# Loading half of W2 ahead of batch 1's v, regrouping the plain blocks of the first chunk, and spreading VectorE's sums of W2

## The chip, the cores and the metric

One core of one Trainium2 chip. The metric is the device time of one execution in microseconds (us). The kernel before takes 278.25 us (median of four runs, 277.8 to 278.66).

Engines by their names in the profile: PE is TensorE, DVE VectorE, ACT ScalarE, POOL GpSimd, SP the engine that here only issues DMAs.

## The reference, cut to what matters

```python
q_s = softmax(q over the head dimension);  k_s = softmax(k over the sequence)
kv = einsum('bhsd,bhse->bhde', k_s, v)            # 8 batches, 8 heads, 576 x 64
x  = einsum('bhsd,bhde->bhse', q_s, kv)           # -> 4608 tokens x 512
h  = x @ w_in                                     # 512 -> 2048
out = (h * sigmoid(h)) @ w_out                    # 2048 -> 512
```

## The kernel before

The tokens go through in chunks of 512. "Chunk 0" is the first (576 wide in its first product, so that batch 0 is whole). A chunk has two products: `mm1` with w_in in 16 blocks, each followed by SiLU (tanh on ScalarE, then a product on VectorE), and the product with w_out (W2). Chunk 0 takes the second product plainly, 16 blocks of four matmuls. From chunk 1 on it is done with seven half-size products instead of eight (the Winograd form of Strassen's scheme), which need sums of the activations (S1 to S4, made for each chunk) and sums of W2 (T1 to T4, made once). T3 overwrites a part of W2.

```python
def t_op(i, eng, f0=0, f1=HF):               # a half of one sum of W2: 128 x 1024 fp16
    o, in0, in1 = {1: (T1, B12, B11), 2: (T2, B22, T1), 3: (T3, B22, B12), 4: (T4, B21, T2)}[i]
    f = slice(f0, f1)
    eng.tensor_tensor(out=o[:, f], in0=in0[:, f], in1=in1[:, f], op=ALU.subtract)

def qnorm(b, cc, eng):                       # row scaling of batch b's softmax of q; GpSimd for most
    ...
    eng.tensor_tensor(out=e, in0=e, in1=r[...].to_broadcast(...), op=ALU.mult)

def silu(t, fb, i, o, w):
    ...
    nc.scalar.activation(out=s, in_=i, func=ACT.Tanh, scale=OS)
    nc.vector.scalar_tensor_tensor(out=o, in0=s, scalar=1.0, in1=i, op0=ALU.add, op1=ALU.mult)   # i is in PSUM

# loads issued by GpSimd, cast to the matmul's types on the way
...
load_w2(0, 4)
load(1, "vt", v, 0, nc.gpsimd)
load(1, "vt", v, 1, nc.gpsimd)
load_w2(4, 8)
...
# TensorE's order: "units"; a plan attaches other work ahead of a unit
units += [lambda i=i: mm2_plain(0, i) for i in range(8)]
for i in range(8, NFB):
    units += [a1[i - 8], lambda i=i: mm2_plain(0, i)]
units += a1[NFB - 8:]                        # a1: the 16 mm1 blocks of chunk 1
...
plan(b1 + 13, lambda: t_op(2, nc.vector, 0, 4))      # b1: the first plain block
plan(b1 + 14, lambda: t_op(2, nc.vector, 4, 8))
plan(b1 + 16, lambda: t_op(4, nc.vector, 0, 4))
plan(b1 + 18, lambda: t_op(4, nc.vector, 4, 8))
...
plan(begin[2] + 5, lambda: t_op(3, nc.vector, 0, 4)) # begin[2]: chunk 2's first mm1 block
plan(begin[2] + 8, lambda: t_op(3, nc.vector, 4, 8))
```

The mm1 blocks of chunk 2 go through three PSUM banks in turn: block n cannot start before VectorE has finished the SiLU product of block n-3.

The softmax here doesn't subtract the row's maximum and nothing guards it: scores larger than these inputs give would overflow.

Of the kernel before, what the change touches and what calls it, by code (L numbers as in the profile page):

```python
# [8 lines left out]
FP32 = mybir.dt.float32  # L9
BF16 = mybir.dt.bfloat16  # L10
FP16 = mybir.dt.float16
ACT = mybir.ActivationFunctionType
# [5 lines left out]
def kernel(  # L18
# [9 lines left out]
    nc = tc.nc  # L28
    B, H, S, D = q.shape
    DM, DFF = w_in.shape  # L30
    NT = B * S
    P = 64
    J = S // P
    NG = H // 2
    NC = DM // 128
    NFB = DFF // 128
# [7 lines left out]
    OS = 0.5 / XS  # L44
# [9 lines left out]
    mp = ctx.enter_context(tc.tile_pool(name="mp", bufs=2))  # L54
# [18 lines left out]
    PS = ps.tile([128, 8, 512], FP32, name="PS")  # L73
# [11 lines left out]
    def copy(eng, o, i):  # L85
        if eng is nc.scalar:
            eng.copy(out=o, in_=i)  # L87
        else:
            eng.tensor_copy(o, i)  # L89

    def load(b, name, src, cc, eng):
        t = ld.tile([128, 2, J * D], FP32, name=name)
        st[b][name, cc] = t
        x = src[b].rearrange("(g r) (p j) d -> g (r p) (j d)", r=2, j=J)
        eng.dma_start(out=t, in_=x.rearrange("g x y -> x g y")[:, 2 * cc:2 * cc + 2, :])

    def jgd(b, name, cc):
        return st[b][name, cc].rearrange("p g (j d) -> p j g d", d=D)

    def half(t, cc):  # L100
        return t[:, :, cc * 128:(cc + 1) * 128].rearrange("p j (g d) -> p j g d", d=D)
# [6 lines left out]
    def exp_k(b, cc):  # L108
        nc.scalar.activation(out=half(ek, cc), in_=jgd(b, "kt", cc), func=ACT.Exp)  # L109

    def vcast(b, cc, eng, g0=0, g1=2):
        o = vaug[:, :, 2 * cc + g0:2 * cc + g1, 0:D]
        i = jgd(b, "vt", cc)[:, :, g0:g1, :]
        copy(eng, o, i)
# [13 lines left out]
    def qsum_end(b, cc):  # L128
        new_zq(b)
        nc.vector.reduce_sum(out=st[b]["zq"][:, cc], in_=st[b]["t2", cc], axis=AX.X)  # L130
        nc.vector.reciprocal(out=st[b]["rzq"][:, cc], in_=st[b]["zq"][:, cc])

    def new_zq(b):
        if "zq" not in st[b]:
            st[b]["zq"] = ap.tile([128, 2, J, 2], FP32, name="zq", bufs=2)
            st[b]["rzq"] = ap.tile([128, 2, J, 2], FP32, name="rzq", bufs=2)
# [11 lines left out]
    def qnorm(b, cc, eng):  # L148
        e = half(st[b]["eq"], cc)
        r = st[b]["rzq"][:, cc]  # L150
        eng.tensor_tensor(  # L151
            out=e, in0=e, in1=r[:, :, :, None].to_broadcast([128, J, 2, D]), op=ALU.mult
        )

    def new_qt(b):
        if "qT" not in st[b]:
            st[b]["qT"] = ap.tile([128, J, 2, 128], BF16, name="qT", bufs=2)
        return st[b]["qT"]

    def q_transpose(b):  # L160
        nc.sync.dma_start_transpose(
            out=new_qt(b).rearrange("x j c y -> x (j c) y"),
            in_=st[b]["eq"].rearrange("x j c -> x (j c)"),
        )

    def tr(b, cc, j0, j1, bank):
        t = PS[:, bank, :].bitcast(BF16)
        for j in range(j0, j1):
            nc.tensor.transpose(
                out=t[:, (j - j0) * 128:(j - j0 + 1) * 128],  # L170
                in_=st[b]["eq"][:, j, cc * 128:(cc + 1) * 128],
                identity=ident,
            )
# [5 lines left out]
    def kv(b, cc):  # L179
        for j in range(J):  # L180
            for r in range(2):
                for s in range(2):
                    nc.tensor.matmul(  # L183
                        out=PS[s * 64:(s + 1) * 64, 6 + r, cc * 128:cc * 128 + E1],
                        lhsT=ek[r * 64:(r + 1) * 64, j, (2 * cc + s) * D:(2 * cc + s + 1) * D],
                        rhs=vaug[r * 64:(r + 1) * 64, j, 2 * cc + s, :],
                        start=(j == 0),
                        stop=(j == J - 1),
                    )
# [13 lines left out]
    def kv_both(b):  # L203
        kv(b, 0)
        kv(b, 1)
        kvcopy(b)
# [25 lines left out]
    def xt(t, cc, eng=nc.scalar):  # L232
        got = pieces(t)
        for b, col, n, dst in got:
            xt_mm(b, cc, col, n, 6, dst)
        xt_evac(t, cc, 6, got[0][3], TCH, got[0][3], eng)
# [30 lines left out]
    hb = [0, 2]  # L267
# [27 lines left out]
    def store(t, col, o):  # L295
        for i in range(2):
            nc.sync.dma_start(out=rows(t, col + i * P), in_=o[i * P:(i + 1) * P, :])

    def mm2_plain(t, fc):
        for tb in range(4):  # L300
            nc.tensor.matmul(  # L301
                out=PS[:, 2 + tb, :],
                lhsT=GTS[t % 2][:, fc, tb * 128:(tb + 1) * 128],
                rhs=W2[:, fc, :],
                start=(fc == 0),
                stop=(fc == NFB - 1),
            )

    def mm2_plain_out(t):
        for ms in ((0, 1), (2, 3)):  # L310
            ow = mp.tile([128, 2, DM], FP32, name="ow", bufs=3)
            for i, m in enumerate(ms):
                if i == 0:
                    nc.scalar.activation(out=ow[:, i], in_=PS[:, 2 + m], func=ACT.Copy, scale=OS)
                else:
                    nc.vector.tensor_scalar_mul(out=ow[:, i], in0=PS[:, 2 + m], scalar1=OS)
                store(t, m * 128, ow[:, i])



# [17 lines left out]
    def t_op(i, eng, f0=0, f1=HF):  # L338
        o, in0, in1 = {
            1: (T1, B12, B11),  # L340
            2: (T2, B22, T1),
            3: (T3, B22, B12),
            4: (T4, B21, T2),
        }[i]
        f = slice(f0, f1)
        eng.tensor_tensor(out=o[:, f], in0=in0[:, f], in1=in1[:, f], op=ALU.subtract)  # L346
# [97 lines left out]
    def load_w2(f0, f1):  # L444
        nc.gpsimd.dma_start(
            out=W2[:, f0:f1, :],
            in_=w_out[f0 * 128:f1 * 128, :].rearrange("(fc p) o -> p fc o", p=128),
        )
# [13 lines left out]
    load(1, "kt", k, 0, nc.gpsimd)  # L462
    load(1, "kt", k, 1, nc.gpsimd)
    load_w2(0, 4)
    load(1, "vt", v, 0, nc.gpsimd)
    load(1, "vt", v, 1, nc.gpsimd)
    load_w2(4, 8)

    qnorm(0, 0, nc.vector)
    qsum(0, 1)  # L470
# [33 lines left out]
    units = []  # L504
    at = {}

    def plan(u, f):
        at.setdefault(u, []).append(f)
# [7 lines left out]
    begin = {1: len(units)}  # L516
# [18 lines left out]
    ORDER = (1, 5, 6, 2, 7, 4, 3)  # L535
    a1 = a_units(1)

    units += [lambda i=i: mm2_plain(0, i) for i in range(8)]
    for i in range(8, NFB):
        units += [a1[i - 8], lambda i=i: mm2_plain(0, i)]  # L540
    units += a1[NFB - 8:]
    for t in range(2, NCH):
        begin[t] = len(units)
        bs = b_units(t - 1, ORDER)
# [72 lines left out]
    b1 = begin[1]  # L617
# [10 lines left out]
    plan(15, lambda: exp_k(1, 1))  # L628
    plan(b1, lambda: (tr(1, 0, 0, 5, 6), tr(1, 0, 5, J, 7)))
    plan(b1, lambda: (trcopy(1, 0, 0, 5, 6, nc.scalar), trcopy(1, 0, 5, J, 7)))  # L630
    plan(b1, lambda: (vcast(1, 0, nc.scalar), qsum_end(1, 1), qnorm(1, 1, nc.vector)))
    plan(b1, lambda: load_w2(12, 16))
    plan(b1, lambda: nc.gpsimd.tensor_copy(GTS[1][:, :, 0:64], GTS[0][:, :, TCH:S]))
    plan(b1, lambda: (load(2, "kt", k, 0, nc.gpsimd), load(2, "kt", k, 1, nc.gpsimd)))
    plan(b1 + 2, lambda: (vcast(1, 1, nc.scalar, 0, 1), vcast(1, 1, nc.vector, 1, 2)))
    plan(b1 + 5, lambda: kv_both(1))
    plan(b1 + 5, lambda: (load(2, "vt", v, 0, nc.gpsimd), load(2, "vt", v, 1, nc.gpsimd)))
    plan(b1 + 6, lambda: (xt(1, 0), tr(1, 1, 0, 5, 0), tr(1, 1, 5, J, 1)))
    plan(b1 + 6, lambda: (trcopy(1, 1, 0, 5, 0, nc.scalar), trcopy(1, 1, 5, J, 1)))
    plan(b1 + 7, lambda: xt(1, 1))  # L640

    plan(b1 + 6, lambda: t_op(1, nc.vector, 0, 4))
    plan(b1 + 7, lambda: t_op(1, nc.vector, 4, 8))
    for i, x in enumerate((8, 10)):
        plan(b1 + x, lambda i=i: exp_q(2, i))
        plan(b1 + x + 1, lambda i=i: qsum(2, i, 0))
        plan(b1 + x + 2, lambda i=i: (qsum(2, i, 1), qnorm(2, i, nc.gpsimd)))
        plan(b1 + x + 5, lambda i=i: exp_k(2, i))
    plan(b1 + 12, lambda: q_transpose(2))
    plan(b1 + 13, lambda: t_op(2, nc.vector, 0, 4))  # L650
    plan(b1 + 14, lambda: t_op(2, nc.vector, 4, 8))
    plan(b1 + 16, lambda: t_op(4, nc.vector, 0, 4))
    plan(b1 + 18, lambda: t_op(4, nc.vector, 4, 8))
    for i, x in enumerate((17, 19)):
        plan(b1 + x, lambda i=i: vcast(2, i, nc.scalar))
    plan(b1 + 20, lambda: loads(3, nc.sync))
    plan(b1 + 21, lambda: kv_both(2))
    plan(b1 + 24, lambda: (mm2_plain_out(0), hb.__setitem__(0, 2), hb.__setitem__(1, 3)))
    for i, x in enumerate((24, 26)):
        plan(b1 + x, lambda i=i: xt(2, i))  # L660
    plan(begin[2] + 5, lambda: t_op(3, nc.vector, 0, 4))
    plan(begin[2] + 8, lambda: t_op(3, nc.vector, 4, 8))

    for t in range(2, NCH - 1):
        b = t + 1
# [58 lines left out]
```

## Time and profile before

I use two lengths, read from TensorE's timeline. **Chunk 1** is the time from the first plain block to the first half-size product with W2. **Chunk 2** is the time from there to the same point one chunk later. Later chunks repeat with 27.78 us.

| | kernel before |
|---|---|
| first plain block / first product / next chunk's | 32.97 / 68.47 / 97.42 us |
| chunk 1 | 35.50 us |
| chunk 2 | 28.95 us, 1.17 over 27.78 |
| TensorE busy | 263.3 us, 95% |

The page of the kernel before. "Busy" is followed by its share of the span. Part 4 is the chain of work that ended last:

```profile
span 276.5 us, 5769 instructions
PE 263.3 (95%) x2343; PEld 168.2 (61%) x2372; DVE 200.5 (73%) x291; ACT 160.3 (58%) x239; POOL 67.3 (24%) x60
...
PE 75%; DMA 9%; DVE 8%; issue 4%; POOL 1%; ACT 1%; POOLq 0%
```

TensorE is the bound, so only its waits can be won. TensorE's timeline of the kernel before, at the three points of the table (the lines from 32.97, 68.47 and 97.42) and at its longest waits in the stretch that the change touches (start, length, what, and in brackets the idle time just before and who ended it):

```profile
32.97 3.62 PE L301 MATMUL PS<-W,GT 128*128 128x512 f16 x16
38.12 1.02 PE L301 MATMUL PS<-W,GT 128*128 128x512 f16 x4 [1.53 <-DMA W<-in_moe_w_out_dram]
...
53.95 0.92 PE L272 MATMUL PS<-XT,W 128*128 128x448 bf16 x4 [1.70 <-DVE GT L245]
...
68.47 1.04 PE L362 MATMUL PS<-W,GT 128*128 128x256 f16 x8
...
80.58 1.02 PE L272 MATMUL PS<-XT,W 128*128 128x512 bf16 x4 [0.66 <-DVE GT L245]
...
82.67 0.81 PE L272 MATMUL PS<-XT,W 128*128 128x512 bf16 x3 [0.19 <-DVE GT L245]
...
97.42 1.04 PE L362 MATMUL PS<-W,GT 128*128 128x256 f16 x8
```

The first wait (38.12) is of the fifth plain block: it waits for W2's second quarter, which by the trace's landing records came at 38.08, after the two loads of v (34.24 and 35.70). The others wait for SiLU products (L245) on VectorE. VectorE's timeline at the same places shows why they are late. L346 is a sum of W2; x2 means two halves merged:

```profile
50.33 3.03 DVE L346 TENSOR_TENSOR T<-W,T 128x1024 f16<-128x1024 f16 x2
...
53.82 0.68 DVE L346 TENSOR_TENSOR T<-W,T 128x1024 f16<-128x1024 f16 x1
...
77.58 2.35 DVE L346 TENSOR_TENSOR W<-W 128x1024 f16<-128x1024 f16 x1
```

And GpSimd's timeline there (L151 is the row scaling, L89 the cast of v):

```profile
48.03 4.18 POOL L151 TENSOR_TENSOR eq<-eq,rzq 128x1152 bf16<-128x1152 bf16 x2 [8.69 <-DVE rzq L146]
75.19 4.19 POOL L151 TENSOR_TENSOR eq<-eq,rzq 128x1152 bf16<-128x1152 bf16 x2 [22.98 <-DVE rzq L146]
79.33 3.71 POOL L89 CAST vaug<-vt 128x1152 bf16<-128x1152 f32 x2
```

A half of a sum takes 0.68 us when GpSimd is idle. The first half of T2 (from 50.33) took 2.43 us and ended 0.55 us after GpSimd's scaling (52.22). The second half of T3 (from 77.58) took 2.35 us and ended 0.55 us after it (79.38). So the sum waits for GpSimd's instruction and only then runs. This is what the Trainium skill tells in "SBUF — State Buffer", section "SBUF: two separate sides": VectorE and GpSimd share a pair of SBUF ports, held for a whole instruction by a GpSimd operation or by a VectorE one with two SBUF inputs (the latter against a GpSimd operation that reads SBUF, as the scaling and the cast do). The trace agrees, by the times above.

### The profile page before, as it was taken

The numbers are of one execution on the slowest core, as the hardware profiler recorded it, in microseconds if no ns is written. First come the engines' busy times: TensorE is split into PE (matmuls) and PEld (weight loads), VectorE is DVE, ScalarE is ACT, GpSimd is POOL, SyncE is SP. The second block draws the span as 40 slices with busy tenths as digits, with TensorE's granted clock in tenths as the row PEclk, the third lists the DMA queues.
The fourth block names the chain that finished last, engine by engine and source line by source line (L and its number), as shares of the span: only waits on it lengthen the run. The fifth ranks groups of instructions, "written<-read, shape, count | busy, mean of one in ns | idle before, by whom it ended". The sixth has DMA issues, their size and how long they took to land.

```text
span 276.5 us, 5769 instructions
## 1 busy us (share of the span) xinstructions
PE 263.3 (95%) x2343; PEld 168.2 (61%) x2372; DVE 200.5 (73%) x291; ACT 160.3 (58%) x239; POOL 67.3 (24%) x60
## 2 busy tenths in 40 slices
PE   8899979799989999999999999999999999999993
PEld 3467634345656566656665666566656665666782
DVE  2867766967998489848984898489937674767643
ACT  5767927777844576457645774577464446444410
POOL 1744960500190009000900090009100000000003
PEclk9999999999999999999999999999999999999999
DMA  7999999599758376937792869241225003300444
GB/s 252 312 201 358 307 284 337 155 305 369 206 147 273 79 175 205 295 80 173 203 297 64 195 196 281 73 104 35 53 44 111 2 0 76 78 0 0 95 98 114
DMA packets 35498, 45.85 MB, mean 166 GB/s; under 512 B 16208, under 2 KB 20048, under 8 KB 35472
## 3 DMA queue, kind: packets, MB, share of 16 engines
q1 hardware_dynamic: 29568, 33.69, 44.3%
q0 software_dynamic: 5584, 11.54, 16.0%
q8 instruction: 18, 0.29, 0.4%
q10 hardware_dynamic: 320, 0.26, 0.3%
q14 instruction: 8, 0.07, 0.1%
HBM read 36.70 MB, written 9.44 MB: 167 GB/s over the span
## 4 chain that ended last, share of the span: by engine, by line
PE 75%; DMA 9%; DVE 8%; issue 4%; POOL 1%; ACT 1%; POOLq 0%
PE PS L272 36%; PE PS L362 34%; DMA W<-in_moe_w_out_dram 5%; DMA W<-in_moe_w_in_dram 4%; PE PS L301 2%; PE PS L222 2%; DVE GT L245 2%; PE PS L183 2%; DVE S L336 1%; POOL W L439 1%; DVE T L346 1%; DVE W L346 1%; DVE zq L144 1%; DVE zq L142 1%; DVE rzq L146 0%
## 5 line engine op out<-in xcount | busy, mean ns | idle before, releaser
L245 DVE SCALAR_TENSOR_TENSOR GT<-sg,PS 128x512 f16<-128x512 f32 (+2 forms) x144 | 96.4, 678 | 54.5 <-ACT sg L244 53.9
L244 ACT ACTIVATE sg<-PS 128x512 f32<-128x512 f32 (+2 forms) x144 | 85.8, 598 | 82.6 <-PE PS L272 75.8
L272 PE MATMUL PS<-XT,W 128*128 128x512 bf16 (+1 forms) x484 | 123.6, 375 | 3.9 <-DVE GT L245 2.6
L272 PEld LDWEIGHTS <-W 128*128 128x128 bf16 x512 | 49.9, 98 | 41.7 <-issue 4.0
L362 PEld LDWEIGHTS <-S 128*128 128x128 f16 x512 | 49.2, 98 | 16.6 <-issue 1.2
L151 POOL TENSOR_TENSOR eq<-eq,rzq 128x1152 bf16<-128x1152 bf16 x13 | 27.4, 2118 | 113.3 <-ACT sg L244 81.6
L362 PEld LDWEIGHTS <-GT 128*128 128x128 f16 x384 | 37.1, 98 | 13.1 <-issue 1.2
L362 PE MATMUL PS<-W,S 128*128 128x256 f16 x256 | 33.0, 273 | 0.1
L362 PE MATMUL PS<-W,GT 128*128 128x256 f16 x256 | 32.7, 273 | 0.1
L362 PE MATMUL PS<-T,S 128*128 128x256 f16 x256 | 32.7, 273 | 0.0
L336 DVE TENSOR_TENSOR S<-GT 128x2048 f16<-128x2048 f16 (+1 forms) x17 | 24.3, 1427 | 0.0
L87 ACT CAST XT<-PS 128x1024 bf16<-128x1024 f32 (+2 forms) x18 | 17.3, 962 | 5.7 <-PE PS L222 5.7
L586 POOL DMA_DIRECT2D out_dram<-ow x4 | 2.2, 550 | 75.7 <-DVE ow L571 75.7
L106 ACT ACTIVATE eq<-qt 128x1152 bf16<-128x1152 f32 x16 | 18.6, 1164 | 2.5 <-DMA qt<-in_q_dram 2.5
L109 ACT ACTIVATE ek<-kt 128x1152 bf16<-128x1152 f32 x16 | 18.6, 1165 | 1.4 <-DMA kt<-in_k_dram 1.4
L142 DVE TENSOR_REDUCE zq<-eq 128x18 f32<-128x1152 bf16 x12 | 16.1, 1344 | 3.8 <-ACT eq L106 3.8
L301 PE MATMUL PS<-W,GT 128*128 128x512 f16 x64 | 16.0, 379 | 1.5 <-DMA W<-in_moe_w_out_dram 1.5
L252 PE MATMUL PS<-XT,W 128*128 128x288 bf16 x128 | 16.5, 286 | 0.7 <-DVE GT L245 0.4
L89 POOL CAST vaug<-vt 128x1152 bf16<-128x1152 f32 x10 | 16.7, 1700 | 0.0
L362 PE MATMUL PS<-T,GT 128*128 128x256 f16 x128 | 16.5, 273 | 0.0
L252 PEld LDWEIGHTS <-W 128*128 128x128 bf16 x128 | 12.4, 98 | 4.7 <-issue 1.7
L336 DVE TENSOR_TENSOR S<-GT,S 128x2048 f16<-128x2048 f16 x8 | 13.1, 1641 | 0.0
(58 smaller groups left out, 158.8 us busy)
## 6 DMA issues: line engine op xcount, KB each, us to landing
out_dram<-ow SPq DMA_DIRECT2D x64, 128.0 KB, 2.4
qt<-in_q_dram SPq DMA_DIRECT2D x12, 576.0 KB, 4.8
kt<-in_k_dram SPq DMA_DIRECT2D x12, 576.0 KB, 6.9
vt<-in_v_dram SPq DMA_DIRECT2D x12, 576.0 KB, 7.6
qt<-in_q_dram POOLq DMA_DIRECT2D x4, 576.0 KB, 13.5
kt<-in_k_dram POOLq DMA_DIRECT2D x4, 576.0 KB, 13.2
vt<-in_v_dram POOLq DMA_DIRECT2D x4, 576.0 KB, 13.6
W<-in_moe_w_out_dram POOLq DMA_DIRECT2D x4, 512.0 KB, 14.6
```

The costliest lines, as they stand in the source:

```text
L87: eng.copy(out=o, in_=i)
L106: nc.scalar.activation(out=half(st[b]["eq"], cc), in_=jgd(b, "qt", cc), func=ACT.Exp)
L109: nc.scalar.activation(out=half(ek, cc), in_=jgd(b, "kt", cc), func=ACT.Exp)
L142: nc.vector.reduce_sum(out=z, in_=e, axis=AX.X)
L151: eng.tensor_tensor(out=e, in0=e, in1=r[:, :, :, None].to_broadcast([128, J, 2, D]), op=ALU.mult)
L244: nc.scalar.activation(out=s, in_=i, func=ACT.Tanh, scale=OS)
L245: nc.vector.scalar_tensor_tensor(out=o, in0=s, scalar=1.0, in1=i, op0=ALU.add, op1=ALU.mult)
L252: nc.tensor.matmul(out=PS[:, 2 * (fb % 3) + n, 0:S // 2], lhsT=W1[:, c, fb * 128:(fb + 1) * 128], rhs=XTS[0][:, c, n * (S // 2):(n + 1) * ...
L272: nc.tensor.matmul(out=PS[:, bank, o0:TCH], lhsT=W1[:, c, fb * 128:(fb + 1) * 128], rhs=XTS[t % 2][:, c, o0:TCH], start=(c == 0), stop=(c ...
L301: nc.tensor.matmul(out=PS[:, 2 + tb, :], lhsT=GTS[t % 2][:, fc, tb * 128:(tb + 1) * 128], rhs=W2[:, fc, :], start=(fc == 0), stop=(fc == N ...
L336: nc.vector.tensor_tensor(out=SS[i - 1][:, f], in0=in0[:, f], in1=in1[:, f], op=op)
L362: nc.tensor.matmul(out=PS[:, bank, m * HN:(m + 1) * HN], lhsT=a[:, fc, m * 128:(m + 1) * 128], rhs=bb[:, fc, :], start=(first and fc == 0) ...
```

## The change

The intent: let W2's second quarter land before TensorE asks for it, use the time in which v is then late for two more plain blocks, leave ten mm1 blocks of chunk 1 as a dense closing stretch, take v's cast for batch 2 off ScalarE, and place the sums of W2 where VectorE seems to have room, after the row sums. No arithmetic is added or removed. The diff's core (cut: the plan lines that move with the new order, among them those of batch 1's casts and batch 2's loads, and the split of the plain output into two halves):

```diff
     load_w2(0, 4)
+    load_w2(4, 8)
     load(1, "vt", v, 0, nc.gpsimd)
     load(1, "vt", v, 1, nc.gpsimd)
-    load_w2(4, 8)
 ...
-    units += [lambda i=i: mm2_plain(0, i) for i in range(8)]
-    for i in range(8, NFB):
-        units += [a1[i - 8], lambda i=i: mm2_plain(0, i)]
-    units += a1[NFB - 8:]
+    units += [lambda i=i: mm2_plain(0, i) for i in range(10)]
+    for i in range(10, NFB):
+        units += [a1[i - 10], lambda i=i: mm2_plain(0, i)]
+    units += a1[NFB - 10:]
 ...
-    plan(b1 + 5, lambda: kv_both(1))
+    plan(b1 + 7, lambda: kv_both(1))
 ...
-    plan(b1 + 13, lambda: t_op(2, nc.vector, 0, 4))
-    plan(b1 + 14, lambda: t_op(2, nc.vector, 4, 8))
-    plan(b1 + 16, lambda: t_op(4, nc.vector, 0, 4))
-    plan(b1 + 18, lambda: t_op(4, nc.vector, 4, 8))
-    for i, x in enumerate((17, 19)):
-        plan(b1 + x, lambda i=i: vcast(2, i, nc.scalar))
+    for i, x in enumerate((16, 18)):
+        plan(b1 + x, lambda i=i: (exp_k(2, i), vcast(2, i, nc.gpsimd)))
+    plan(b1 + 18, lambda: t_op(2, nc.vector, 0, 4))
+    plan(b1 + 20, lambda: t_op(2, nc.vector, 4, 8))
 ...
-    plan(begin[2] + 5, lambda: t_op(3, nc.vector, 0, 4))
-    plan(begin[2] + 8, lambda: t_op(3, nc.vector, 4, 8))
+    plan(begin[2] + 7, lambda: t_op(4, nc.vector, 0, 4))
+    plan(begin[2] + 8, lambda: t_op(4, nc.vector, 4, 8))
+    plan(begin[2] + 12, lambda: t_op(3, nc.vector, 0, 4))
+    plan(begin[2] + 13, lambda: t_op(3, nc.vector, 4, 8))
```

More of the change, by code (lines that the diff above doesn't have):

```diff
@@ L307, in mm2_plain, with mm2_plain_out @@
             )
-    def mm2_plain_out(t):
-        for ms in ((0, 1), (2, 3)):
-            ow = mp.tile([128, 2, DM], FP32, name="ow", bufs=3)
-            for i, m in enumerate(ms):
-                if i == 0:
-                    nc.scalar.activation(out=ow[:, i], in_=PS[:, 2 + m], func=ACT.Copy, scale=OS)
-                else:
-                    nc.vector.tensor_scalar_mul(out=ow[:, i], in0=PS[:, 2 + m], scalar1=OS)
-                store(t, m * 128, ow[:, i])
+    def mm2_plain_out(t, ms):
+        ow = mp.tile([128, 2, DM], FP32, name="ow", bufs=3)
+        for i, m in enumerate(ms):
+            if i == 0:
+                nc.scalar.activation(out=ow[:, i], in_=PS[:, 2 + m], func=ACT.Copy, scale=OS)
+            else:
+                nc.vector.tensor_scalar_mul(out=ow[:, i], in0=PS[:, 2 + m], scalar1=OS)
+            store(t, m * 128, ow[:, i])
     WG = [dict() for _ in range(NCH)]
@@ L630 @@
     plan(b1, lambda: (trcopy(1, 0, 0, 5, 6, nc.scalar), trcopy(1, 0, 5, J, 7)))
-    plan(b1, lambda: (vcast(1, 0, nc.scalar), qsum_end(1, 1), qnorm(1, 1, nc.vector)))
+    plan(b1, lambda: (qsum_end(1, 1), qnorm(1, 1, nc.vector)))
     plan(b1, lambda: load_w2(12, 16))
+    plan(b1, lambda: (load(2, "kt", k, 0, nc.gpsimd), load(2, "kt", k, 1, nc.gpsimd)))
+    plan(b1, lambda: (load(2, "vt", v, 0, nc.gpsimd), load(2, "vt", v, 1, nc.gpsimd)))
     plan(b1, lambda: nc.gpsimd.tensor_copy(GTS[1][:, :, 0:64], GTS[0][:, :, TCH:S]))
-    plan(b1, lambda: (load(2, "kt", k, 0, nc.gpsimd), load(2, "kt", k, 1, nc.gpsimd)))
-    plan(b1 + 2, lambda: (vcast(1, 1, nc.scalar, 0, 1), vcast(1, 1, nc.vector, 1, 2)))
-    plan(b1 + 5, lambda: kv_both(1))
-    plan(b1 + 5, lambda: (load(2, "vt", v, 0, nc.gpsimd), load(2, "vt", v, 1, nc.gpsimd)))
-    plan(b1 + 6, lambda: (xt(1, 0), tr(1, 1, 0, 5, 0), tr(1, 1, 5, J, 1)))
-    plan(b1 + 6, lambda: (trcopy(1, 1, 0, 5, 0, nc.scalar), trcopy(1, 1, 5, J, 1)))
-    plan(b1 + 7, lambda: xt(1, 1))
-    plan(b1 + 6, lambda: t_op(1, nc.vector, 0, 4))
-    plan(b1 + 7, lambda: t_op(1, nc.vector, 4, 8))
-    for i, x in enumerate((8, 10)):
+    plan(b1 + 4, lambda: vcast(1, 0, nc.scalar))
+    plan(b1 + 5, lambda: (tr(1, 1, 0, 5, 0), tr(1, 1, 5, J, 1)))
+    plan(b1 + 5, lambda: (vcast(1, 1, nc.scalar, 0, 1), vcast(1, 1, nc.vector, 1, 2)))
+    plan(b1 + 6, lambda: (trcopy(1, 1, 0, 5, 0, nc.scalar), trcopy(1, 1, 5, J, 1)))
+    plan(b1 + 7, lambda: kv_both(1))
+    plan(b1 + 8, lambda: xt(1, 0))
+    plan(b1 + 9, lambda: xt(1, 1))
+    plan(b1 + 8, lambda: t_op(1, nc.vector, 0, 4))
+    plan(b1 + 9, lambda: t_op(1, nc.vector, 4, 8))
+    for i, x in enumerate((10, 12)):
         plan(b1 + x, lambda i=i: exp_q(2, i))
@@ L647 @@
         plan(b1 + x + 2, lambda i=i: (qsum(2, i, 1), qnorm(2, i, nc.gpsimd)))
-        plan(b1 + x + 5, lambda i=i: exp_k(2, i))
-    plan(b1 + 12, lambda: q_transpose(2))
-    plan(b1 + 13, lambda: t_op(2, nc.vector, 0, 4))
-    plan(b1 + 14, lambda: t_op(2, nc.vector, 4, 8))
-    plan(b1 + 16, lambda: t_op(4, nc.vector, 0, 4))
-    plan(b1 + 18, lambda: t_op(4, nc.vector, 4, 8))
-    for i, x in enumerate((17, 19)):
-        plan(b1 + x, lambda i=i: vcast(2, i, nc.scalar))
+    plan(b1 + 14, lambda: q_transpose(2))
+    for i, x in enumerate((16, 18)):
+        plan(b1 + x, lambda i=i: (exp_k(2, i), vcast(2, i, nc.gpsimd)))
+    plan(b1 + 18, lambda: t_op(2, nc.vector, 0, 4))
+    plan(b1 + 20, lambda: t_op(2, nc.vector, 4, 8))
     plan(b1 + 20, lambda: loads(3, nc.sync))
-    plan(b1 + 21, lambda: kv_both(2))
-    plan(b1 + 24, lambda: (mm2_plain_out(0), hb.__setitem__(0, 2), hb.__setitem__(1, 3)))
-    for i, x in enumerate((24, 26)):
+    plan(b1 + 22, lambda: (mm2_plain_out(0, (0, 1)), hb.__setitem__(0, 2), hb.__setitem__(1, 3)))
+    plan(b1 + 23, lambda: kv_both(2))
+    for i, x in enumerate((25, 28)):
         plan(b1 + x, lambda i=i: xt(2, i))
-    plan(begin[2] + 5, lambda: t_op(3, nc.vector, 0, 4))
-    plan(begin[2] + 8, lambda: t_op(3, nc.vector, 4, 8))
+    plan(b1 + 30, lambda: mm2_plain_out(0, (2, 3)))
+    plan(begin[2] + 7, lambda: t_op(4, nc.vector, 0, 4))
+    plan(begin[2] + 8, lambda: t_op(4, nc.vector, 4, 8))
+    plan(begin[2] + 12, lambda: t_op(3, nc.vector, 0, 4))
+    plan(begin[2] + 13, lambda: t_op(3, nc.vector, 4, 8))
     for t in range(2, NCH - 1):
```

## The prediction

> **What bounds the kernel.** TensorE: busy 95% of 276.5 us, and 75% of the chain that ended last. Chunks 3 to 6 repeat every 27.78 us, nearly gapless. The change touches only 33 to 96 us. There the timeline of TensorE shows these losses:
> - 1.53 us at 36.6: the fifth plain block waits for the second quarter of W2, landed at 38.08. GpSimd's loads land in order of issue, about 1.5 us apart for 576 KB and 2.4 us for W2; the two loads of v for batch 1 (34.24, 35.70) stand before it.
> - 1.70 us at 52.2, by VectorE: a sum of W2 took 2.43 us instead of 0.68, while GpSimd ran the row scaling (2 x 2.11 us).
> - Chunk 2 took about 29.1 us instead of 27.78; waits of 0.66 and 0.19 us on VectorE, after T3's second sum took 2.35 us, again beside the scaling.
>
> The Trainium skill, "SBUF — State Buffer", section "SBUF: two separate sides", tells of a port pair held exclusively for a whole instruction by either a GpSimd operation or a VectorE one with two SBUF inputs. The trace agrees: each long sum ends about 0.55 us after GpSimd's instruction.
>
> **What changes, costed.** No arithmetic is removed.
> 1. W2's second quarter should land near 35.1, v near 36.6 and 38.1, the third quarter still at 40.7. The 1.53 us wait goes. Eight plain blocks (0.87 us each) with transposes, kv and xt reach block 8 at about 41.5, so no new wait on W2.
> 2. Ten plain blocks first: at the first block of chunk 1 (43.9 in both) two more plain blocks are done: 1.7 us gained.
> 3. T2 moves behind the row sums and apart. I expect its halves still to meet GpSimd (scaling until about 52, then v's casts, 1.16 us each alone), at about 1.6 and 1.2 us. v's casts of batch 2 move from ScalarE to GpSimd, end near 55.5, and make kv(2) wait about 0.7 us; ScalarE's copy of bank 2 costs about 0.4 us before the first of the ten closing blocks. These ten run near 0.76 us each. Chunk 2 then starts near 63.9 instead of 66.7: about 2.8 us gained.
> 4. T4 moves into chunk 2, where VectorE is already 92 to 99% busy (windows 70:80 and 80:90). T4's halves stand right behind each row sum's scaling on GpSimd, so each should take about 2.3 us instead of 0.68, and S3 and T3 meet v's casts. With three banks for the SiLU products TensorE then waits some 3 to 4 us in chunk 2 instead of about 1.3: 2 to 3 us given back.
>
> Everything later should be unchanged, shifted. Net: about 0.8 us gained, all on the critical path.
>
> **Time:** 277.8 us, 275.2 to 280.4 in 8 of 10. Faster by over 2%: 0.04; within 2%: 0.92; slower: 0.04. The touched stretch's waits sum to about 5.3 us, 1.9%, so over 2% is hardly to be had.
>
> **What would show it.** Step 1: no wait of TensorE on W2; landing near 35. Step 2: ten plain blocks done by about 43.8. Step 3: chunk 2's first block near 64; T2 halves above 1 us; a wait before kv(2). Step 4: T4 halves near 2.3 us, TensorE waits on VectorE's SiLU products in chunk 2 of over 2 us, chunk 2 over 30 us. Period of 27.78 us afterwards.
>
> **What would make it wrong.** If T4's halves miss the scaling (0.68 us each), or the waits fall in VectorE's slack, chunk 2 costs no more than before, and the time is about 275.5. If kv(2) waits for late casts by 2 us or more, or T3 comes late for its products, the time passes 279.

## More of the kernel before

All runs told here are with a granted TensorE clock of 0.99 to 1.00. Later sets ran on other chips of the kind, each with its own runs of the kernel before beside it, so each experiment is compared with the kernel before of its own set.

## The result, and the profile after

The changed kernel takes 277.13 us (median of four runs, 276.93 to 277.29) against 278.25 (277.8 to 278.66). The ratio is 0.996, 95% interval 0.9939 to 0.9981. (A ratio here is the mean time of one kernel's fast runs over that of the other's of the same rounds, so not quite the ratio of the medians quoted.) That is a small gain, clear of noise.

| | before | after | difference |
|---|---|---|---|
| first plain block | 32.97 | 32.84 | -0.13 |
| chunk 1 | 35.50 | 32.46 | -3.04 |
| chunk 2 | 28.95 | 31.04 | +2.09 |
| chunk 3 | 27.78 | 27.78 | 0 |
| median time | 278.25 | 277.13 | -1.12 |

The first three differences sum to -1.08 us; the spans of the two profiled executions differ by 1.2 us and the medians by 1.12. So the account is complete to about 0.1 us: 3.0 us won in chunk 1, and two thirds of it given back in chunk 2. One caution: the lengths come from one execution of each kernel. The wait for W2, 1.53 us here, was 1.05 and 1.11 us in two later profiles (e12, e13) that are alike up to there. So chunk 1's gain is sure to a few tenths only.

The page of the changed kernel, the lines that answer to those of before:

```profile
span 275.3 us, 5801 instructions
PE 266.0 (97%) x2372; PEld 168.3 (61%) x2372; DVE 201.5 (73%) x291; ACT 158.3 (57%) x237; POOL 70.6 (26%) x62
...
PE 85%; DVE 9%; ACT 2%; DMA 1%; POOL 1%; issue 1%; POOLq 0%
```

The DMA's share of the chain fell from 9% to 1%; VectorE's went from 8% to 9%. Such a share is no saving: before, the chain ran through 26 us of loads, on which TensorE waited only 1.53 us at the end. (The busy time of PE did not really rise. 29 matmul records are missing from the trace before, 2343 against 2372, and most of them are mm1 blocks.) TensorE's timeline, its waits in the same stretch and the three points of the table (the lines from 32.84, 65.30 and 96.34):

```profile
32.84 4.49 PE L301 MATMUL PS<-W,GT 128*128 128x512 f16 x20
...
53.98 0.92 PE L272 MATMUL PS<-XT,W 128*128 128x448 bf16 x4 [0.26 <-ACT ow L313]
...
65.30 1.04 PE L361 MATMUL PS<-W,GT 128*128 128x256 f16 x8
...
76.22 1.02 PE L272 MATMUL PS<-XT,W 128*128 128x512 bf16 x4 [1.20 <-DVE GT L245]
...
79.08 1.02 PE L272 MATMUL PS<-XT,W 128*128 128x512 bf16 x4 [0.97 <-DVE GT L245]
...
81.17 1.02 PE L272 MATMUL PS<-XT,W 128*128 128x512 bf16 x4 [0.19 <-DVE GT L245]
...
96.34 1.04 PE L361 MATMUL PS<-W,GT 128*128 128x256 f16 x8
```

Both long waits of chunk 1 (1.53 and 1.70) are gone; 0.26 us on ScalarE is new. That makes 2.97 of chunk 1's 3.04 us. The waits for SiLU products in chunk 2 grew from 0.85 to 2.36 us (listed are those over 0.15 us; the lengths of the chunks hold the shorter ones too). VectorE's timeline says what stood in front of them (line 345 is now the sum of W2):

```profile
50.71 1.90 DVE L345 TENSOR_TENSOR T<-W,T 128x1024 f16<-128x1024 f16 x1
...
53.07 1.10 DVE L345 TENSOR_TENSOR T<-W,T 128x1024 f16<-128x1024 f16 x1
...
71.71 2.35 DVE L345 TENSOR_TENSOR T<-W,T 128x1024 f16<-128x1024 f16 x1
...
76.08 2.35 DVE L345 TENSOR_TENSOR T<-W,T 128x1024 f16<-128x1024 f16 x1
```

GpSimd at these places:

```profile
47.87 4.19 POOL L151 TENSOR_TENSOR eq<-eq,rzq 128x1152 bf16<-128x1152 bf16 x2 [7.26 <-DVE rzq L146]
52.01 3.18 POOL L89 CAST vaug<-vt 128x1152 bf16<-128x1152 f32 x2
71.40 2.12 POOL L151 TENSOR_TENSOR eq<-eq,rzq 128x1152 bf16<-128x1152 bf16 x1 [16.21 <-ACT sg L244]
75.77 2.12 POOL L151 TENSOR_TENSOR eq<-eq,rzq 128x1152 bf16<-128x1152 bf16 x1 [2.25 <-DVE rzq L146]
```

Each half of T4 (71.71, 76.08) starts 0.31 us after a scaling on GpSimd (71.40, 75.77) and lasts until 0.54 us after its end. That is no accident. A row sum on VectorE (its reciprocal ended at 71.25 and 75.63) releases the scaling on GpSimd, and the sum of W2 stands one SiLU product later in VectorE's order: "behind the row sums" is just where GpSimd is busy.

### The profile page after: what moved, and what is told of

Same layout as the page of the kernel before. It is cut to its first block, busy times and chain, and to the rows that moved or that the text cites. A ratio compares the mean times of both kernels' runs of the same rounds, so it can differ in the third digit from the quotient of the medians.

```text
span 275.3 us, 5801 instructions
## 1 busy us (share of the span) xinstructions
PE 266.0 (97%) x2372; PEld 168.3 (61%) x2372; DVE 201.5 (73%) x291; ACT 158.3 (57%) x237; POOL 70.6 (26%) x62
## 4 chain that ended last, share of the span: by engine, by line
PE 85%; DVE 9%; ACT 2%; DMA 1%; POOL 1%; issue 1%; POOLq 0%
PE PS L272 38%; PE PS L361 34%; PE PS L301 5%; PE PS L252 4%; PE PS L222 2%; PE PS L183 2%; DVE zq L142 2%; DVE T L345 2%; DVE GT L245 2%; DVE S L335 1%; DMA qt<-in_q_dram 1%; DVE eq L151 1%; ACT eq L106 1%; ACT sg L244 1%; POOL t L120 0%
## 5 line engine op out<-in xcount | busy, mean ns | idle before, releaser
L272 PE MATMUL PS<-XT,W 128*128 128x512 bf16 (+1 forms) x512 | 126.5, 376 | 2.6 <-DVE GT L245 2.4
L89 POOL CAST vaug<-vt 128x1152 bf16<-128x1152 f32 x12 | 19.9, 1686 | 0.0
```

What stands on the lines that cost most here:

```text
L89: eng.tensor_copy(o, i)
L272: nc.tensor.matmul(out=PS[:, bank, o0:TCH], lhsT=W1[:, c, fb * 128:(fb + 1) * 128], rhs=XTS[t % 2][:, c, o0:TCH], start=(c == 0), stop=(c ...
```

## The experiments

Twelve kernels ran (no run has the number e6); all gave correct results. The theory: chunk 1 gained because TensorE no longer waits for W2 or for the sums, and chunk 2 lost because T4's halves meet GpSimd's row scaling at the port. Rivals: the load order alone is worth its wait; chunk 2 simply has too many operations on VectorE; or chunk 1's gain is only apparent. No run moves T2 alone, or the order of the plain blocks alone: that the sums of W2 no longer hold up chunk 1 is read from the timelines above. The summary, with times of each against the kernel before of its own set:

| run | time (before in its set) | chunk 1 | chunk 2 |
|---|---|---|---|
| before / after | 278.25 / 277.13 | 35.50 / 32.46 | 28.95 / 31.04 |
| e1: before, W2 ahead of v only | 277.88 (277.97) | 35.10 | 28.95 |
| e2: after, v ahead again | 278.39 (277.97) | 33.35 | 31.05 |
| e3: after, T4 before the row sums | 275.37 (277.97) | 32.45 | 29.38 |
| e4: after, T4 in the closing blocks | 274.16 (277.97) | 32.46 | 28.17 |
| e5: after, T3 and T4 on GpSimd | **273.85** (278.09) | 32.46 | 27.78 |
| e7: after, v's casts on ScalarE | 278.04 (278.09) | 33.64 | 31.07 |
| e8: after, T3 and T4 in the closing blocks | 274.40 (278.09) | 33.06 | 27.78 |
| e9: e5 and another bank | 274.95 (278.09) | 33.66 | 27.78 |
| e10: e9, loads later | 275.16 (278.00) | 33.66 | 27.78 |
| e11: e5, loads later | 273.98 (278.00) | 32.45 | 27.78 |
| e12: before, T3 on GpSimd | 280.60 (278.00) | 38.38 | 27.78 |
| e13: before, T3 in the last blocks of chunk 1 | 276.99 (278.34) | 35.29 | 27.78 |

### Load order alone, and undone (e1, e2)

```diff
 # e1, from the kernel before; e2 undoes the same in the changed kernel
     load_w2(0, 4)
+    load_w2(4, 8)
     load(1, "vt", v, 0, nc.gpsimd)
     load(1, "vt", v, 1, nc.gpsimd)
-    load_w2(4, 8)
```

> The kernel before, with W2's second quarter loaded ahead of batch 1's v and nothing else changed. Theory (the early load pays only with the later use of v): the fifth plain block no longer waits, but v then lands near 36.8 and 38.3 instead of 34.2 and 35.7, and kv of batch 1, still before the sixth block, which TensorE reaches near 37.3, waits about 1.7 us. Time within 0.5 us of the kernel before. Rival (the load order alone is worth its wait): 1.5 us faster than the kernel before.

> The changed kernel with v ahead of W2's second quarter again, as in the kernel before. Theory: the fifth plain block waits about 1.5 us for W2 near 36.5, nothing later absorbs it, and the time is about 278.6, 1.5 us over the changed kernel. Rival (VectorE bounds the stretch, a wait of TensorE at its start costs nothing): time as the changed kernel's, within 0.4 us.

e1 took 277.88 us beside 277.97, ratio 0.9989, 95% interval 0.9972 to 1.0005: no gain to be told from noise. The second quarter of W2 landed at 34.99 and v at 36.52 and 37.99, as expected. The wait moved to kv, in two parts (0.46 and 0.49 us; I had said 1.7). PE's waits in e1:

```profile
PE PS L183 <- ACT vaug L87: 0.9, 2, 0.5
```

e2 took 278.39 us, ratio 1.0014, where the changed kernel in its own set stood at 0.996: about 1.5 us given up (0.0054 of 278 us), as expected. The wait for W2 is back, 0.7 us by the profile (1.5 expected; chunk 1 grew by 0.89, and in this profile the first plain block started 0.25 us later as well):

```profile
PE PS L301 <- DMA W<-in_moe_w_out_dram: 0.7, 1, 0.7
```

So in the changed kernel the load order is worth 0.9 us of chunk 1 in the profile, about 1.5 us by the times; in the kernel before it is worth nothing that the times show. The reading is that it pays only with the plain blocks regrouped so that kv comes later; no run separates the regrouping from the rest of the change. Both waits were smaller than I had said.

### Where T4 stands (e3, e4)

```diff
 # e3
-    plan(begin[2] + 7, lambda: t_op(4, nc.vector, 0, 4))
-    plan(begin[2] + 8, lambda: t_op(4, nc.vector, 4, 8))
+    plan(begin[2] + 5, lambda: t_op(4, nc.vector, 0, 4))
+    plan(begin[2] + 5, lambda: t_op(4, nc.vector, 4, 8))
 # e4: the same two lines at b1 + 25 and b1 + 28
```

> The changed kernel with both halves of T4 just ahead of batch 3's first row sum, in the same chunk: as many operations on VectorE in chunk 2, but GpSimd idle beside T4. Theory (the port held by GpSimd costs the time): both halves take 0.68 us instead of 2.35, chunk 2 loses about 1.3 us against 27.78 instead of 3.3, time about 275.1. Rival (chunk 2 has simply too many operations on VectorE): chunk 2 stays near 31 us and the time near 277.1.

> The changed kernel with the halves of T4 among the ten closing blocks of chunk 1, where GpSimd is idle and VectorE has gaps of about 2.4 us in all. Theory: both halves take 0.68 us, the closing blocks cost at most 0.3 us more, chunk 2 loses about 0.5 us against 27.78, and the time is about 274.4. Rival (VectorE's work there delays the SiLU products and chunk 2's first sums by as much): time 276.5 or more.

e3 is the one that separates the port from the amount of work: chunk 2 has the same operations on VectorE, in another order. VectorE's timeline in e3 (the two halves of T4 merged, then S3, a sum of activations, which now meets the scaling, then the halves of T3):

```profile
69.59 1.29 DVE L345 TENSOR_TENSOR T<-W,T 128x1024 f16<-128x1024 f16 x2
...
75.59 2.29 DVE L335 TENSOR_TENSOR S<-GT 128x2048 f16<-128x2048 f16 x1
...
78.41 2.59 DVE L345 TENSOR_TENSOR W<-W 128x1024 f16<-128x1024 f16 x2
```

TensorE's longest wait in e3's chunk 2:

```profile
81.05 0.60 PE L361 MATMUL PS<-W,S 128*128 128x256 f16 x4 [0.94 <-DVE W L345]
```

Two halves took 1.29 us together instead of 4.70, chunk 2 fell from 31.04 to 29.38, and the time to 275.37 (ratio 0.9901). The rival that the amount of work on VectorE alone makes the loss is out: the same work, 1.66 us less. But the amount is not free. Chunk 2 of e3 still takes 1.60 us over 27.78 (1.3 expected), and its longest wait is for T3, whose halves met the casts of v. e4 takes T4 out of chunk 2; its halves in the closing blocks:

```profile
58.43 0.68 DVE L345 TENSOR_TENSOR T<-W,T 128x1024 f16<-128x1024 f16 x1
...
61.15 0.68 DVE L345 TENSOR_TENSOR T<-W,T 128x1024 f16<-128x1024 f16 x1
```

Chunk 1 is as long as in the changed kernel (32.46), chunk 2 is 28.17, and the time is 274.16 (ratio 0.9859). Of the 3.26 us that chunk 2 of the changed kernel loses against 27.78, T4 at its place makes 2.87: 1.66 by standing beside the scaling (e3), and another 1.21 by standing in chunk 2 at all (e3 against e4). The latter is about the 1.29 us that its halves take when nothing holds them up; T3's halves met the casts in e4 as well (2.60 us together), and there it cost TensorE no such wait.

### Sums of W2 on GpSimd, or all on VectorE in the closing blocks (e5, e8)

```diff
 # e5
-    plan(begin[2] + 7, lambda: t_op(4, nc.vector, 0, 4))
-    plan(begin[2] + 8, lambda: t_op(4, nc.vector, 4, 8))
-    plan(begin[2] + 12, lambda: t_op(3, nc.vector, 0, 4))
-    plan(begin[2] + 13, lambda: t_op(3, nc.vector, 4, 8))
+    plan(b1 + 24, lambda: t_op(4, nc.gpsimd, 0, 4))
+    plan(b1 + 25, lambda: t_op(4, nc.gpsimd, 4, 8))
+    plan(b1 + 26, lambda: t_op(3, nc.gpsimd, 0, 4))
+    plan(b1 + 27, lambda: t_op(3, nc.gpsimd, 4, 8))
 # e8: T4 at b1 + 25 and 28, T3 at b1 + 30 and 31, all on nc.vector
```

> The changed kernel with T4 and T3 computed by GpSimd itself during the ten closing blocks of chunk 1, where it stands idle (55.2 to 71.4 us in the changed kernel). Theory: at the 1.83 ns for an element a partition that its row scaling shows, four halves take about 1.9 us each and end near 63, before VectorE's first two-input sum near 66.7; VectorE's SiLU products, which read PSUM, are not slowed (0.62 us); chunk 2 has no wait over 0.2 us and takes 27.8 to 28.0; time about 273.8. Rival (GpSimd is slower at it, or VectorE is slowed beside it): ends after 66, S1 is held up, time 275 or more.

> As the run with T4 among the closing blocks, and T3 there too, all on VectorE, with GpSimd idle. Theory: all four halves take 0.68 us; VectorE, whose gaps there came to 2.4 us, is now full and passes up to 0.4 us on to the start of chunk 2, which then takes 27.8 to 28.0 us instead of 28.2; time 273.8 to 274.3. Rival (VectorE's work in the closing blocks now delays them): time over 274.8.

e5 has the lowest time: 273.85 us (273.72 to 273.98) beside 278.09, ratio 0.985, 95% interval 0.9835 to 0.9865. (By the times it can't be told from e4, 0.9842 to 0.9875, or from e11; that its chunk 2 is 0.39 us shorter than e4's is seen in the profiles.) GpSimd's timeline in e5:

```profile
51.99 3.18 POOL L89 CAST vaug<-vt 128x1152 bf16<-128x1152 f32 x2
55.13 4.21 POOL L345 TENSOR_TENSOR T<-W,T 128x1024 f16<-128x1024 f16 x2
59.29 4.21 POOL L345 TENSOR_TENSOR W<-W 128x1024 f16<-128x1024 f16 x2
71.38 4.22 POOL L151 TENSOR_TENSOR eq<-eq,rzq 128x1152 bf16<-128x1152 bf16 x2 [7.87 <-ACT sg L244]
```

A half takes GpSimd 2.12 us (1.9 expected) against VectorE's 0.68, and it does not matter: GpSimd has nothing else to do from 55 to 71 us. VectorE's SiLU products of 128x448 beside it took 0.62 us, as they do in the changed kernel without it; they read one operand from PSUM. Chunk 2 is 27.78 us, like every later chunk. e8 does the same on VectorE and is 0.6 us longer in chunk 1 (33.06): VectorE was full there, and TensorE waited 0.6 us on a SiLU product. 274.40 us; slightly more than expected.

### v's casts back on ScalarE (e7)

```diff
-        plan(b1 + x, lambda i=i: (exp_k(2, i), vcast(2, i, nc.gpsimd)))
+        plan(b1 + x, lambda i=i: exp_k(2, i))
+        plan(b1 + x + 1, lambda i=i: vcast(2, i, nc.scalar))
```

> The changed kernel with the casts of batch 2's v on ScalarE again, at the places of the kernel before. Theory (order on ScalarE): the first cast waits there for v, landed at 50.55, and both casts stand before tanh of blocks that TensorE needs, and before the copy of bank 2; T2's second half no longer meets GpSimd (0.68 us), but TensorE loses 1 to 2 us by ScalarE before the closing blocks; time about 278.5. Rival (the cast on GpSimd costs more by the port than it saves): time 276.7 or less.

278.04 us beside 278.09, ratio 1.0001, so about 1.1 us over the changed kernel (0.996 in its set). ScalarE's timeline in e7:

```profile
50.73 1.17 ACT L87 CAST vaug<-vt 128x1152 bf16<-128x1152 f32 x1 [0.46 <-DMA vt<-in_v_dram]
...
53.28 1.15 ACT L87 CAST vaug<-vt 128x1152 bf16<-128x1152 f32 x1
...
54.76 0.59 ACT L313 ACTIVATE ow<-PS 128x512 f32<-128x512 f32 x1
```

The copy of bank 2 (L313) came 1.4 us later than in the changed kernel (54.76 against 53.34), and TensorE waited 1.6 us for it instead of 0.3. So in the order of the changed kernel this part is worth about 1 us, though the casts on GpSimd cost T2's second half 0.4 us (1.10 against 0.68).

### A free bank, and later loads (e9, e10, e11)

```diff
 # e9, from e5: the first closing block stays on bank 0
-    plan(b1 + 22, lambda: (mm2_plain_out(0, (0, 1)), hb.__setitem__(0, 2), hb.__setitem__(1, 3)))
+    plan(b1 + 22, lambda: mm2_plain_out(0, (0, 1)))
+    plan(b1 + 23, lambda: (hb.__setitem__(0, 1), hb.__setitem__(1, 3)))
 # e10: e9, and e11: e5, with
-    plan(b1 + 20, lambda: loads(3, nc.sync))
+    plan(b1 + 24, lambda: loads(3, nc.sync))
```

> As the run with T3 and T4 on GpSimd, and the first closing block keeps to its free bank 0, with the switch to three banks one block later, so that it need not wait for ScalarE's copy of bank 2 (0.26 us by the profile of the changed kernel, 0.4 us between its neighbours). Theory: 0.3 to 0.4 us faster than that run, if nothing else in the closing blocks then waits. Rival: the wait moves to the casts before kv of batch 2, no gain (within 0.1 us).

> As the run with T3 and T4 on GpSimd and the free bank 0, and the loads of batch 3 issued four units later. In the run without that, q's transposition for batch 2 landed 6.4 us after its issue instead of 4.7, and TensorE waited 1.0 us for it. Theory (those loads, issued 2.9 us after it, delayed its end): it lands within 4.8 us, the wait goes, and the time is 273.5 to 273.8. Rival (the transposition is late for another reason): time stays near 274.9.

> Control: the run with T3 and T4 on GpSimd (bank 2 as in the changed kernel), with the loads of batch 3 four units later alone. Expected: no change from its 273.85, within 0.2 us, since its transposition already landed in 4.66 us and batch 3's q is used only near 67.7 us.

e9 was meant to win the last 0.3 us and lost 1.1 instead: 274.95 (ratio 0.9892), consistently in four runs. The wait on ScalarE is gone, and others came, in PE's waits:

```profile
PE PS L222 <- DMA qT<-eq: 1.0, 1, 1.0
PE PS L183 <- POOL vaug L89: 0.4, 1, 0.4
```

The second I had named as the rival; the first I had not foreseen. The trace's semaphore records show that of the 16 increments of q's transposition fifteen came by 56.65 us and the last at 58.29 (in e5 all came by 56.72). My theory for it fell: with the loads issued at 57.86 instead of 54.80 us (e10) the last increment still came 1.67 us after the fifteenth; 275.16 us (ratio 0.9902). The control e11 changed nothing, as expected: 273.98 (ratio 0.9855). A 16 KB packet of the instruction queue runs on a DMA engine at 56.16 us in e9, but such a packet is there in e5 as well. Why one DMA engine is late stays open.

### What chunk 2 could have gained by itself (e12, e13)

```diff
 # e12, from the kernel before
-    plan(begin[2] + 5, lambda: t_op(3, nc.vector, 0, 4))
-    plan(begin[2] + 8, lambda: t_op(3, nc.vector, 4, 8))
+    plan(b1 + 25, lambda: t_op(3, nc.gpsimd, 0, 4))
+    plan(b1 + 26, lambda: t_op(3, nc.gpsimd, 4, 8))
 # e13: the same two lines at b1 + 28 and b1 + 30, on nc.vector
```

> The kernel before with only T3 moved to GpSimd, at the end of chunk 1. It separates what the changed kernel gained in chunk 1 from what chunk 2 could have gained by itself. Theory: chunk 2 goes from 29.1 to 27.8 us and chunk 1 stays as it is, so 1.2 to 1.4 us under the kernel before, and the rest of the way to 273.85 is the rearranged chunk 1 (about 3.0 us). Rival (chunk 1's gain was illusory and came from the lighter chunk 2): 274.5 or less.

> The kernel before with T3 on VectorE among the last blocks of chunk 1, where GpSimd has nothing to do (the run with T3 on GpSimd failed to separate the two: GpSimd started at once, beside T2 and T4). Theory: T3's halves take 0.68 us each, chunk 2 goes from 29.1 to 27.8 us, chunk 1 loses at most 0.3 us: 1.0 to 1.4 us under the kernel before, near 276.8. What then remains to the best kernel (273.85), about 3 us, is chunk 1's new order. Rival (chunk 1's gain came from the lighter chunk 2): 275 or less.

e12 missed: 280.60 us (279.52 to 281.12), ratio 1.0097. Chunk 2 did become 27.78, but chunk 1 grew by 2.9. A plan orders work within each engine, it does not hold an engine back. I had thought that T3 must wait for the plain blocks whose W2 it overwrites; but it overwrites rows that only the first eight blocks read. So GpSimd began at once:

```profile
51.44 5.08 POOL L346 TENSOR_TENSOR W<-W 128x1024 f16<-128x1024 f16 x2
```

and VectorE's sums of T2 and T4 met it:

```profile
49.59 4.95 DVE L346 TENSOR_TENSOR T<-W,T 128x1024 f16<-128x1024 f16 x2
...
55.00 2.07 DVE L346 TENSOR_TENSOR T<-W,T 128x1024 f16<-128x1024 f16 x1
```

TensorE waited 3.6 us. The same collision, made by accident and larger. e13 is the repaired one: 276.99 us beside 278.34, ratio 0.9958, chunk 2 27.78 and chunk 1 35.29. So chunk 2 holds 1.2 us of gain for the kernel before, and no more. The rival that chunk 1's gain was only apparent is out: from e13 to e5 chunk 2 is the same and chunk 1 is 2.83 us shorter.

## Why the prediction was right or wrong

The time (277.8 predicted, 277.13 measured) and the mechanism held. The predicted range, 275.2 to 280.4, also holds the time of the kernel before, so the time alone tests little; the steps are the test. Point by point:

1. *W2's second quarter near 35.1, the wait gone, the third quarter no new wait.* Right: landings 35.31, 36.82 and 38.30 for v, 40.71 for the third quarter, and no wait of TensorE on W2. e2 shows that this part is needed, e1 that it is not enough alone.
2. *Two more plain blocks done by 43.9.* Right: the first mm1 block of chunk 1 began at 43.77 after ten plain blocks (before: 43.93 after eight).
3. *Chunk 2 near 63.9; T2's halves 1.6 and 1.2 us; kv(2) waits 0.7 us; ScalarE's copy costs 0.4 us.* Mostly right: 1.90 and 1.10 us; 0.26 us by the profile for the copy; chunk 2's first mm1 block, the start that the prediction counts from, began at 63.46 (before: 66.74). Wrong in size: kv(2) waited about 0.1 us (it began 54.83 us, right behind its neighbour). I had made all of kv(2) wait for the second cast, but its first half needs only the first cast, and the second cast ended at 55.19 instead of 55.5. The ten closing blocks missed the other way: from 53.98 to 63.46, without kv and xt, they took 0.79 to 0.80 us each instead of 0.76. So it is partly luck that the sum of step 3 came out so near.
4. *T4's halves 2.3 us each, waits of 3 to 4 us in chunk 2 instead of 1.3, 2 to 3 us given back.* Right: 2.35 us each, 3.26 against 1.17 us over 27.78, 2.09 given back. S3 and T3 did meet v's casts: 1.56 us for S3 and 1.64 for T3's two halves, against 1.22 and 1.29 alone. e3 and e4 show that of the 2.87 us that T4 costs in chunk 2 the collision with the scaling makes 1.66; the rest stays as long as T4 is in that chunk.
5. *Net 0.8 us, later chunks unchanged.* 1.1 us, and chunk 3 is 27.78 in both.

The term that was off is the net: a difference of two terms of 2 to 3 us, each off by a few tenths. The chance of 0.04 for over 2% was sound for this change: even the best variant, with no wait over 0.3 us left in either chunk, is 1.5% faster.

## What to carry to other kernels

When a change moves the time little, split the timeline at points that every version passes and subtract: here +3.0 and -2.1 us stood behind a gain of 0.4%, and the second term could be undone by moving two lines. Before placing a VectorE operation with two SBUF inputs, look at what GpSimd does at that moment, above all when the same VectorE instruction stream has just released it; either run it before the release (e3), or put it into a stretch where GpSimd is idle (e4), or give it to GpSimd there, even at three times the duration (e5). A place in an engine's order is not a time: check what the operation really waits for (e12), and expect a won wait to uncover another (e1, e9).

## What the Trainium skill lacked or had wrong

- "SBUF — State Buffer", section "SBUF: two separate sides", says that the later of the two fully blocks. All runs agree (0.68 us against 2.35). It says that whichever starts first gets the ports, and does not spell out what happens when GpSimd's instructions follow each other closely: VectorE's operation, which had waited since before the second one, got in between (a half of T2 from 50.71 us ended at 52.61, between the scaling's end at 52.06 and the cast's at 53.63). Nor does that section say outright that a recorded duration includes the wait, on either engine: the same cast of v on GpSimd took 1.16 us where no VectorE operation with two SBUF inputs stood in its way and up to 2.15 where one did.
- "GPSIMD Engine Reference", section "4.1 Engine selection", puts elementwise work with two inputs on GpSimd at about twice VectorE's time and names no element type there. Here a fp16 subtraction of 128x1024 took 2.12 us against 0.68, 3.1 times, so twice is too low for this fp16 operation. With GpSimd idle that did no harm (e5).
- "DMA: Bandwidth & Descriptors", section "Why a DMA increments its semaphore by 16 and not by 1", says that the engines of a DMA finish independently. It gives no idea of the spread: in e9 and e10 the last of the transposition's 16 increments came 1.6 to 1.7 us after the fifteenth, in the changed kernel all 16 came within 0.11 us. No run explains that.
